# Attention with hash-routed experts: routing computed beside the first batch, row tables three pairs behind their one-hots

## The chip, the cores and the metric

The kernel runs on one core of one Trainium2 chip. The metric is the device time of one launch in microseconds, the median over several runs. A core has TensorE (PE: matmuls and transposes), VectorE (DVE), ScalarE (ACT), GpSimd (POOL) and SyncE (SP); each works through its own list of instructions in the order in which they were written down, and waits where an input or a buffer isn't ready. Loads and stores are started by SP, ACT or POOL and carried out by 16 DMA engines.

## What is computed

```python
B, H, S, D = 8, 8, 576, 64            # attention, block-causal with blocks of 64
scores = (q @ k^T) / sqrt(D);  mask = (row // 64) >= (col // 64)
x = softmax(masked scores) @ v        # -> x: [4608, 512], a row per token

E, F = 8, 1024                        # experts: 512 -> 1024 -> 512
expert_idx = token_ids * 2654435761 % E
out[rows of e] = relu(x[rows of e] @ w1[e]) @ w2[e]
```

Inputs are 32-bit floats, the token ids 64-bit integers. The multiplier is odd, and the kernel needs only the lowest three bits of each id: as 2654435761 leaves the remainder 1 when divided by 8, the expert is the id modulo 8.

## The kernel before

The kernel has two stages. The attention works on **pairs of heads**: 8 batches of 4 pairs, 32 pairs in all, numbered g = 4b + pr. The experts follow, once x has been written to device memory.

For one pair, the chain is as follows. Q and K are loaded as 32-bit values, cast to bf16 (`cast_qk`: rows 0 to 511 on VectorE, the "rest" rows 512 to 575 on GpSimd), transposed on TensorE (`T_pair`, L231; the rest rows of a whole batch by `T_rest`, L206) and copied from PSUM into `qkT` by VectorE (L236, L212). `S_chunk` (L243 to L289) makes the scores of a pair in three chunks, and ScalarE turns each chunk into exponentials `pt` (L289). `S_rest` does the same for the rest rows of a batch. `PV` (L326) multiplies them with V, to which a column of ones is added so that the row sums come with the product, and `norm` (L343, L346) divides by these sums on VectorE. V is cast by GpSimd (`cast_v`, L183 to L188, and `cast_v4`, L194). `write_x` sends a finished batch to `x_dram` from GpSimd's queue.

The order is written out by hand in one loop over g. In step g, the scores of pair g are interleaved with PV of pair g-2; then come the transposes of pair g+2, V casts of pair g+3, one routing step, and the casts of Q and K of the next batch. PSUM for the output of PV exists once (`psO`, one buffer), so PV of a pair waits for the norm of the one before it. The tiles for transposes, `psT`, rotate through two buffers, and the small routing products use them too. Loads go to SyncE's queue; each of Q, K and V has two 32-bit buffers, so a load for batch b+2 starts when batch b has been cast.

**The routing** (`route`, a generator whose parts are separated by `yield`) finds for every token a slot in a table sorted by expert. Its parts are: the expert of each token (L373 to L386, with a small transposing matmul at L381); the one-hot over experts (L394); a running count and the counts per expert, with two matmuls (L400 to L411); the overflow arithmetic, which moves tokens beyond the 640 slots of an expert into extra tiles (L415 to L436); the split of each slot into a column and a lane, `shi` and `slo` (L440 to L448); and the list of overflow tiles (L452 to L462). `rows` prepares row numbers in two digits, `vhi` and `vlo` (L467 to L481).

**The row table** says which row of x belongs in which slot. For each batch, `place_a` makes one-hots of the lanes and columns on VectorE (L490, L493) and multiplies the latter with the row digits on GpSimd (L496, L499). `place_b` multiplies the two on TensorE (L509) and adds the product to `acc` (L512). `placed` turns the sum into the index table `perm3`, by which the experts' rows are gathered and written. Where the steps stand in the loop is given by the dictionary `steps`: routing parts at the end of g = 2 to 8, `rows` at 7, `place_a` of batch j at 11 + 2j, `place_b` at 12 + 2j, `placed` at 27.

After the loop, the rows of each expert are gathered from `x_dram`, transposed, multiplied with w1 and w2, and written to their places. This part isn't touched by the diff. The functions that are:

Of the kernel before, what the change touches and what calls it, by code (L numbers as in the profile page):

```python
# [7 lines left out]
ALU = mybir.AluOpType  # L8
# [12 lines left out]
B, H, S, D = 8, 8, 576, 64  # L21
E, DM, FF = 8, 512, 1024
N = B * S
NT = 4
NP = H // 2
CAP = 640
# [8 lines left out]
def kernel(  # L35
# [10 lines left out]
    nc = tc.nc  # L46
    P = nc.NUM_PARTITIONS
# [49 lines left out]
    def load_qk(b, h0=0, h1=H, rest=True, main=True, engs=None):  # L97
        if b not in loaded:
            loaded[b] = [ld.tile([P, 36, D], F32, name="qf", tag="qf"),
                         ld.tile([P, 36, D], F32, name="kf", tag="kf"), None]  # L100
        for w, src in ((0, q), (1, k)):
            t = loaded[b][w]
            eng = engs[w] if engs else nc.sync
            if main and w == 0:
                eng.dma_start(
                    t[:, 4 * h0 : 4 * h1, :].rearrange("p (h c) d -> p h (c d)", c=4),
                    src[b, h0:h1, 0:512, :].rearrange("h (p c) d -> p h (c d)", c=4),
                )
            elif main:
                for r in range(2):  # L110
                    eng.dma_start(
                        t[:, 4 * h0 : 4 * h1, :].rearrange(
                            "p (h r c) d -> p h r (c d)", r=2, c=2)[:, :, r],
                        src[b, h0:h1, 256 * r : 256 * r + 256, :].rearrange("h (p c) d -> p h (c d)", c=2),
                    )
            if rest:
                for g in range(2):
                    eng.dma_start(
                        t[64 * g : 64 * g + 64, 32:36, :],
                        src[b, 4 * g : 4 * g + 4, 512:576, :].rearrange("h r d -> r h d"),  # L120
                    )
# [41 lines left out]
    def cast_qk(b, which, r0=0, r1=NP, rest=True):  # L163
        src = loaded[b][which]
        cb = casted.setdefault(b, {})
        if which not in cb:
            cb[which] = att.tile([P, 36, D], BF16, name="qb" if which == 0 else "kb",
                                 tag="qb" if which == 0 else "kb")
        dst = cb[which]
        if r1 > r0:  # L170
            nc.vector.tensor_copy(  # L171
                dst[:, 8 * r0 : 8 * r1, :].rearrange("p (r c m) d -> p r m c d", c=4, m=2),
                src[:, 8 * r0 : 8 * r1, :].rearrange("p (r m c) d -> p r m c d", c=4, m=2),
            )
        if rest:
            nc.gpsimd.tensor_copy(dst[:, 32:36, :], src[:, 32:36, :])
# [13 lines left out]
    def cast_v4(b):  # L190
        vf = loaded[b][2]
        vx, v4 = vexts[b % 2]
        for m in range(2):
            nc.gpsimd.tensor_copy(  # L194
                v4[64 * m : 64 * m + 64, :, m, 0:D], vf[64 * m : 64 * m + 64, 32:36, :])
# [165 lines left out]
    tid = rt.tile([B, S], I64, name="tid")  # L361
# [8 lines left out]
    def route():  # L370
# [8 lines left out]
        for i in range(5):  # L379
# [8 lines left out]
        T = 5 * B  # L388
# [30 lines left out]
        inc = rt.tile([P, E], F32, name="inc")  # L419
        nc.vector.tensor_tensor_scan(inc[:], ovf[:], ovf[:], 0.0, op0=ALU.add, op1=ALU.bypass)  # L420
        e640 = rt.tile([P, E], F32, name="e640")
        nc.vector.tensor_single_scalar(e640[:], iota_e[:], float(CAP), op=ALU.mult)

        off1 = rt.tile([P, E], F32, name="off1")
        nc.vector.tensor_tensor(out=off1[:], in0=base[:, 0, :], in1=offs[:], op=ALU.subtract)
        off2 = rt.tile([P, E], F32, name="off2")
        nc.vector.tensor_tensor(out=off2[:], in0=inc[:], in1=ovf[:], op=ALU.subtract)
        nc.vector.tensor_scalar(off2[:], off2[:], 128.0, float(E * CAP - CAP), op0=ALU.mult, op1=ALU.add)
        nc.vector.tensor_tensor(out=off2[:], in0=off2[:], in1=e640[:], op=ALU.subtract)
        nc.vector.tensor_tensor(out=cum[:], in0=cum[:], in1=off1[:, :, None].to_broadcast([P, E, T]), op=ALU.add)  # L430
        ovm = rt.tile([P, E, T], F32, name="ovm")
        nc.vector.tensor_single_scalar(ovm[:], cum[:], float(CAP) + 0.5, op=ALU.is_gt)
        nc.vector.tensor_tensor(out=ovm[:], in0=ovm[:], in1=off2[:, :, None].to_broadcast([P, E, T]), op=ALU.mult)
        nc.vector.tensor_tensor(out=cum[:], in0=cum[:], in1=ovm[:], op=ALU.add)
        nc.vector.tensor_tensor(out=cum[:], in0=cum[:], in1=e640[:, :, None].to_broadcast([P, E, T]), op=ALU.add)
        nc.vector.scalar_tensor_tensor(out=cum[:], in0=cum[:], scalar=-1.0, in1=oh[:],  # L436
                                       op0=ALU.add, op1=ALU.mult)
        yield
        slf = rt.tile([P, T], F32, name="slf")
        nc.vector.tensor_reduce(slf[:], cum[:].rearrange("p e t -> p t e"), axis=AX.X, op=ALU.add)  # L440
# [45 lines left out]
    def place_a(b):  # L486
        ohp = rt.tile([P, 5, P], BF16, name="ohp", tag="ohp", bufs=2)
        ohs = rt.tile([P, 5, NG], BF16, name="ohs", tag="ohs", bufs=2)
        ohg = rt.tile([P, 5, 2, NG], BF16, name="ohg", tag="ohg", bufs=2)
        nc.vector.tensor_tensor(  # L490
            out=ohp[:], in0=iota_p[:, None, :].to_broadcast([P, 5, P]),
            in1=slo[:, b, :, None].to_broadcast([P, 5, P]), op=ALU.is_equal)
        nc.vector.tensor_tensor(  # L493
            out=ohs[:], in0=iota_p[:, None, 0:NG].to_broadcast([P, 5, NG]),
            in1=shi[:, b, :, None].to_broadcast([P, 5, NG]), op=ALU.is_equal)
        nc.gpsimd.tensor_tensor(  # L496
            out=ohg[:, :, 0, :], in0=ohs[:],
            in1=vhi[:, b, :, None].to_broadcast([P, 5, NG]), op=ALU.mult)
        nc.gpsimd.tensor_tensor(  # L499
            out=ohg[:, :, 1, :], in0=ohs[:],  # L500
            in1=vlo[:, :, None].to_broadcast([P, 5, NG]), op=ALU.mult)
        places[b] = (ohp, ohg)

    def place_b(b):
        ohp, ohg = places.pop(b)
        pq = psT.tile([P, 512], F32, name="pq", tag="tp")
        for i in range(5):
            n = P if i < NT else 64
            nc.tensor.matmul(pq[:, 0 : 2 * NG], lhsT=ohp[0:n, i, :],  # L509
                             rhs=ohg[0:n, i, :, :].rearrange("p w g -> p (w g)"),  # L510
                             start=(i == 0), stop=(i == 4))
        nc.vector.tensor_tensor(out=acc[:].rearrange("p w g -> p (w g)"),  # L512
                                in0=acc[:].rearrange("p w g -> p (w g)"), in1=pq[:, 0 : 2 * NG], op=ALU.add)
# [26 lines left out]
    NPAIRS = B * NP  # L540
    both = (nc.sync, nc.scalar)
    load_qk(0, 0, 2, rest=False, engs=both)
    load_qk(0, main=False, engs=both)
    load_qk(0, 2, 8, rest=False, engs=both)
    load_v(0)
    nc.sync.dma_start(tid[:], moe_token_ids.rearrange("(b s) -> b s", b=B))
    load_qk(1)
    load_v(1)
    rgen = route()
# [3 lines left out]
    for w in range(2):  # L553
        cast_qk(0, w, 0, 0)
    T_rest(0)
    for w in range(2):
        cast_qk(0, w, 1, 2, rest=False)

    steps = {g: (lambda: next(rgen, None)) for g in range(2, 9)}
    steps[7] = rows  # L560
    for j in range(B):
        steps[11 + 2 * j] = lambda j=j: place_a(j)
        steps[12 + 2 * j] = lambda j=j: place_b(j)
    steps[27] = placed
    for g in range(NPAIRS + 2):
        b, pr = divmod(g, NP)
        live = g < NPAIRS
        nxt = live and b + 1 < B
        if live:
            S_chunk(g, 0)  # L570
        if g >= 2:
            PV(g - 2, 0)
        if live:
            S_chunk(g, 1)
        if g >= 2:
            PV(g - 2, 1)
            norm(g - 2)
        if live:
            S_chunk(g, 2)
            if pr == 0:  # L580
                S_rest(b)
        if g == 0:
            T_pair(1)
        if g < 2:
            for w in range(2):
                cast_qk(0, w, g + 2, g + 3, rest=False)
        if g + 2 < NPAIRS:
            T_pair(g + 2)
        for gv in range(NP) if g == 0 else (g + 3,):
            bv, pv = divmod(gv, NP)  # L590
            if bv < B:
                cast_v(bv, pv)
                if pv == 0:
                    cast_v4(bv)
        if g in steps:
            steps[g]()
        if nxt:
            if pr == 0:
                cast_qk(b + 1, 0, 0, 2)
            elif pr == 1:  # L600
                cast_qk(b + 1, 1, 0, 2)
            elif pr == 2:
                T_rest(b + 1)
                cast_qk(b + 1, 0, 2, 4, rest=False)
            else:
                cast_qk(b + 1, 1, 2, 4, rest=False)
        if pr == 1 and b >= 1:
            write_x(b - 1)
        if pr == (1 if b == 0 else 0) and b + 2 < B:
            load_qk(b + 2)  # L610
            load_v(b + 2)
        if 6 <= g < 6 + 2 * G:
            nc.gpsimd.memset(xgs[g - 6][:], 0.0)
        if pr == 0 and b == 6:
            load_w1(0)
        if pr == 0 and b == 7:
            load_w2(0)
# [161 lines left out]
```

The softmax here doesn't subtract the row's maximum and nothing guards it: scores larger than these inputs give would overflow.

## Time and profile before

| what | value |
|---|---|
| median of 3 runs | 345.86 us (343.06 to 347.33) |
| profiled span | 343.6 us |
| first exponential of the attention | 9.96 us |
| last exponential starts its run of five at | 152.66 us |
| first gather of expert rows | 171.27 us |
| busy: PE, DVE, ACT, POOL | 81%, 46%, 42%, 58% |

The page divides the span into 40 slices. Below, each digit is the busy share of a slice in tenths, and PEclk is the clock that was granted to TensorE, in tenths of the full one:

```profile
PE   1574784998878888895039989999999999999991
DVE  4345769888868788863020224040413324040330
ACT  1342762887657577783004440604133140604100
POOL 3065378388988789960374647274664737232352
PEclk9997886999989899997558999999999999999998
DMA  7999997899898984672226987796969697825432
```

The attention fills the first 18 slices and a part of the next. In the first six of these, none of TensorE, VectorE, ScalarE and GpSimd is full. From the twenty-second slice on, TensorE is full with the experts' matmuls. In a list in order of time, each row has the start in us, the time in us, the engine, the line, the operation, what it writes and reads, and in brackets how long the engine sat idle before it and what released it. In a table of windows, each row has the window, its length, the busy time of each engine with the number of instructions, the mean granted clock, the share of the DMA engines and the rate.

### The profile page before, as it was taken

Reading aid. Unit: us, or ns where it says so; the run is one execution under the profiler, and the core shown is the slowest. Engines: PE = TensorE matmul, PEld = TensorE weight load, DVE = VectorE, ACT = ScalarE, POOL = GpSimd, SP = SyncE. Lnnn points to the kernel's source line nnn. Section 1 sums busy time; section 2 is a strip of 40 time slices with the busy share of each in tenths; the row PEclk is TensorE's granted clock in tenths of the full one; section 3 lists DMA queues with packets and bytes.
Section 4 is the critical chain, followed back from the end, with each engine's and each line's share of the span. In section 5 each row is a group of like instructions: output and inputs, shape, how many; then the busy total and the mean of one; then the engine's idle time right before and its main releaser. Section 6 shows DMA issues by size and latency. Waiting matters only on the chain. (4 is left out here: it accounts for less than half of the span.)

```text
span 343.6 us, 7894 instructions
## 1 busy us (share of the span) xinstructions
PE 277.1 (81%) x3247; PEld 201.2 (59%) x3247; DVE 158.8 (46%) x346; ACT 142.8 (42%) x169; POOL 198.1 (58%) x281
## 2 busy tenths in 40 slices
PE   1574784998878888895039989999999999999991
PEld 1342663776656666664028865949586685949540
DVE  4345769888868788863020224040413324040330
ACT  1342762887657577783004440604133140604100
POOL 3065378388988789960374647274664737232352
PEclk9997886999989899997558999999999999999998
DMA  7999997899898984672226987796969697825432
GB/s 200 284 272 283 246 273 173 216 280 268 211 288 184 285 184 78 138 134 72 69 85 126 215 194 240 167 215 176 200 203 186 231 175 225 194 77 134 129 130 75
DMA packets 67045, 64.58 MB, mean 188 GB/s; under 512 B 19378, under 2 KB 60340, under 8 KB 64960
## 3 DMA queue, kind: packets, MB, share of 16 engines
q0 software_dynamic: 12288, 35.71, 43.5%
q1 hardware_dynamic: 52064, 27.17, 32.4%
q10 hardware_dynamic: 2656, 1.18, 1.3%
q8 instruction: 26, 0.43, 0.5%
q14 instruction: 11, 0.09, 0.1%
HBM read 67.15 MB, written 15.20 MB: 240 GB/s over the span
## 5 line engine op out<-in xcount | busy, mean ns | idle before, releaser
L289 ACT ACTIVATE pt<-ps 128x1024 bf16<-128x1024 f32 x96 | 94.3, 1022 | 54.3 <-PE ps L265 54.0
L662 ACT ACTIVATE hT<-hp 128x640 bf16<-128x640 f32 x64 | 45.0, 703 | 117.1 <-PE hp L657 117.1
L657 PE MATMUL hp<-xT,w1b 128*128 128x320 bf16 x512 | 72.7, 303 | 0.6 <-DVE xT L646 0.6
L657 PEld LDWEIGHTS <-w1b 128*128 128x128 bf16 x512 | 69.9, 144 | 3.2 <-issue 1.1
L672 PE MATMUL yp<-w2b,hT 128*128 128x512 bf16 x320 | 70.2, 379 | 0.0
L679 POOL DMA_INDIRECT out_dram<-ysb,perm x40 | 39.7, 992 | 35.6 <-DVE ysb L677 26.8
L646 DVE COPY xT<-tpx 128x512 bf16<-128x512 bf16 x40 | 15.7, 422 | 79.4 <-PE tpx L645 77.4
L672 PEld LDWEIGHTS <-hT 128*128 128x128 bf16 x320 | 31.0, 98 | 36.2
L677 DVE COPY ysb<-yp 128x512 f32<-128x512 f32 x40 | 27.7, 692 | 51.7 <-PE yp L672 51.7
L633 POOL DMA_INDIRECT xg<-x_dram,perm x40 | 40.6, 1015 | 16.5 <-issue 11.9
L326 PE MATMUL O<-vx,pt 128*128 128x65 bf16 x896 | 43.7, 206 | 2.6 <-DVE xs L346 2.2
L243 PE MATMUL ps<-qkT 64*128 64x64 bf16 (+2 forms) x384 | 37.9, 280 | 2.6 <-ACT pt L289 2.2
L326 PEld LDWEIGHTS <-pt 128*128 128x128 bf16 x896 | 35.8, 105 | 6.4 <-issue 1.8
L183 POOL CAST vx<-vf 128x512 bf16<-128x512 f32 x32 | 21.1, 669 | 20.9 <-DMA vf<-in_v_dram 19.9
L645 PE MATMUL tpx<-identbf,xg 128*128 128x128 bf16 x160 | 15.0, 229 | 19.9 <-DMA xg<-x_dram,perm 16.7
L356 POOL DMA_DIRECT2D x_dram<-xs x32 | 23.3, 734 | 13.1 <-DVE xs L346 12.6
L346 DVE TENSOR_TENSOR xs<-O,rs 128x320 bf16<-128x320 f32 x64 | 28.4, 486 | 1.1
L265 PE MATMUL ps<-maskq,maskk 64*128 64x64 bf16 (+1 forms) x256 | 28.3, 214 | 0.0
L645 PEld LDWEIGHTS <-xg 128*128 128x128 bf16 x160 | 11.0, 101 | 23.7 <-DMA xg<-x_dram,perm 18.0
L236 DVE COPY qkT<-tp 128x1024 bf16<-128x1024 bf16 x32 | 22.0, 688 | 5.0 <-PE tp L231 4.0
L531 POOL DMA_DIRECT2D w1b<-in_moe_w_dram x8 | 4.9, 614 | 30.8 <-PE tpx L645 26.7
L231 PE MATMUL tp<-identbf,qb 128*128 128x128 bf16 x128 | 13.7, 233 | 8.2 <-DVE qb L171 8.0
(112 smaller groups left out, 264.3 us busy)
## 6 DMA issues: line engine op xcount, KB each, us to landing
vf<-in_v_dram SPq DMA_DIRECT2D x16, 512.0 KB, 7.1
w1b<-in_moe_w_dram POOLq DMA_DIRECT2D x8, 1024.0 KB, 8.1
w2b<-in_moe_w_dram POOLq DMA_DIRECT2D x8, 1024.0 KB, 8.6
qf<-in_q_dram SPq DMA_DIRECT2D x7, 1024.0 KB, 7.9
kf<-in_k_dram SPq DMA_DIRECT2D x14, 512.0 KB, 7.1
x_dram<-xs POOLq DMA_DIRECT2D x32, 128.0 KB, 5.8
qf<-in_q_dram SPq DMA_DIRECT2D x16, 64.0 KB, 6.7
vf<-in_v_dram SPq DMA_DIRECT2D x16, 64.0 KB, 5.8
```

What stands on the lines that cost most here:

```text
L243: nc.tensor.matmul(ps[:, m, o0 : o0 + n], lhsT=qk[rows, pr, 1, 128 * kt : 128 * kt + 128], rhs=qk[rows, pr, 0, q0 : q0 + n], start=first, ...
L265: nc.tensor.matmul(ps[:, m, o0 : o0 + 128 * n].rearrange("p (t h j) -> p t h j", h=2, j=16)[:, :, 0, :], lhsT=maskk[rows, c, :], rhs=maskq ...
L289: nc.scalar.activation(ptv[:, :, 512 * ch : 512 * ch + 512], ps[:], ACT.Exp, scale=SCALE)
L326: nc.tensor.matmul(O[:, t, :], lhsT=pt[:, m * PTW + o0 : m * PTW + o0 + 128], rhs=vx[:, h, i, :], start=(n == 0), stop=(n == t),)
L346: nc.vector.tensor_tensor(out=xs[:, :, 0:DM].rearrange("p t (d h k) -> p h t d k", d=4, h=H)[:, h], in0=O[:, m, :, 0:D].rearrange("p t (k ...
L633: nc.gpsimd.indirect_dma_start(out=xgs[g % (2 * G)][:], out_offset=None, in_=x_dram[:, :], in_offset=bass.IndirectOffsetOnAxis(ap=perm3[:, ...
L645: nc.tensor.transpose(out=tp[:, db, :], in_=xg[:, db * P : (db + 1) * P], identity=identbf[:])
L657: nc.tensor.matmul(hp[:, t, 0:HC], lhsT=w1b[:, db, ft::NFT], rhs=xT[:, db, t * HC : (t + 1) * HC], start=(db == 0), stop=(db == NKT - 1),)
L662: nc.scalar.activation(hT[:, ft, :].rearrange("p (t n) -> p t n", t=2), hp[:, :, 0:HC], ACT.Relu)
L672: nc.tensor.matmul(yp[:], lhsT=hT[:, ft, tt * P : (tt + 1) * P], rhs=w2b[:, ft, :], start=(ft == 0), stop=(ft == NFT - 1),)
L677: nc.vector.tensor_copy(ysb[:], yp[:])
L679: ins = nc.gpsimd.indirect_dma_start(out=out[:, :], out_offset=bass.IndirectOffsetOnAxis(ap=perm3[:, gg : gg + 1], axis=0), in_=ysb[:], in ...
```

## The change

Four things are changed. The token ids are loaded on ScalarE's queue right after the first K rows instead of behind V on SyncE's. The routing parts are brought forward: the first three into step 0, the overflow arithmetic to the end of step 1, the split into columns and lanes to step 2, and the overflow list and `rows` to step 3. The purpose is to use the time in which VectorE waits for the first batch's loads. The overflow arithmetic is fused: the constant -1 is folded into two small operations, and the comparison with the capacity and the multiplication become one operation.

The row tables start earlier, `place_a` of batch j at 5 + 2j, and `place_b` follows at 8 + 2j, three pairs later instead of one, so that TensorE doesn't reach the product before its factors are ready. Last, the casts of Q and K for the next batch, with the rest rows on GpSimd, and the routing steps now stand ahead of the V casts in each step of the loop, so that the rest casts don't queue behind V casts that wait for their load. In step 0, `cast_v4` comes after the V casts.

```diff
-        nc.vector.tensor_single_scalar(e640[:], iota_e[:], float(CAP), op=ALU.mult)
+        nc.vector.tensor_scalar(e640[:], iota_e[:], float(CAP), -1.0, op0=ALU.mult, op1=ALU.add)
...
-        nc.vector.tensor_single_scalar(ovm[:], cum[:], float(CAP) + 0.5, op=ALU.is_gt)
-        nc.vector.tensor_tensor(out=ovm[:], in0=ovm[:], in1=off2[:, :, None].to_broadcast([P, E, T]), op=ALU.mult)
+        nc.vector.scalar_tensor_tensor(
+            out=ovm[:], in0=cum[:], scalar=float(CAP) + 0.5,
+            in1=off2[:, :, None].to_broadcast([P, E, T]), op0=ALU.is_gt, op1=ALU.mult)
...
-        nc.vector.scalar_tensor_tensor(out=cum[:], in0=cum[:], scalar=-1.0, in1=oh[:],
-                                       op0=ALU.add, op1=ALU.mult)
+        nc.vector.tensor_tensor(out=cum[:], in0=cum[:], in1=oh[:], op=ALU.mult)
...
     load_qk(0, 0, 2, rest=False, engs=both)
+    nc.scalar.dma_start(tid[:], moe_token_ids.rearrange("(b s) -> b s", b=B))
     load_qk(0, main=False, engs=both)
     load_qk(0, 2, 8, rest=False, engs=both)
     load_v(0)
-    nc.sync.dma_start(tid[:], moe_token_ids.rearrange("(b s) -> b s", b=B))
...
-    steps = {g: (lambda: next(rgen, None)) for g in range(2, 9)}
-    steps[7] = rows
+    steps = {g: [] for g in range(NPAIRS + 2)}
+    steps[1].append(lambda: next(rgen))
+    steps[2].append(lambda: next(rgen))
+    steps[3] += [lambda: next(rgen, None), rows]
     for j in range(B):
-        steps[11 + 2 * j] = lambda j=j: place_a(j)
-        steps[12 + 2 * j] = lambda j=j: place_b(j)
-    steps[27] = placed
+        steps[5 + 2 * j].append(lambda j=j: place_a(j))
+        steps[8 + 2 * j].append(lambda j=j: place_b(j))
+    steps[23].append(placed)
...
         if g == 0:
+            next(rgen)
+            for w in range(2):
+                cast_qk(0, w, 1, 2, rest=False)
             T_pair(1)
+            next(rgen)
...
-        for gv in range(NP) if g == 0 else (g + 3,):
-            bv, pv = divmod(gv, NP)
-            if bv < B:
-                cast_v(bv, pv)
-                if pv == 0:
-                    cast_v4(bv)
-        if g in steps:
-            steps[g]()
+        if g == 0:
+            next(rgen)
+            for pv in range(NP):
+                cast_v(0, pv)
+            cast_v4(0)
...
+        for step in steps[g]:
+            step()
+        bv, pv = divmod(g + 3, NP)
+        if 0 < bv < B:
+            cast_v(bv, pv)
+            if pv == 0:
+                cast_v4(bv)
```

More of the change, by code (lines that the diff above doesn't have):

```diff
@@ L427, in route @@
         nc.vector.tensor_tensor(out=off2[:], in0=inc[:], in1=ovf[:], op=ALU.subtract)
-        nc.vector.tensor_scalar(off2[:], off2[:], 128.0, float(E * CAP - CAP), op0=ALU.mult, op1=ALU.add)
+        nc.vector.tensor_scalar(off2[:], off2[:], 128.0, float(E * CAP - CAP - 1), op0=ALU.mult, op1=ALU.add)
         nc.vector.tensor_tensor(out=off2[:], in0=off2[:], in1=e640[:], op=ALU.subtract)
@@ L555 @@
     T_rest(0)
-    for w in range(2):
-        cast_qk(0, w, 1, 2, rest=False)
-    steps = {g: (lambda: next(rgen, None)) for g in range(2, 9)}
-    steps[7] = rows
+    steps = {g: [] for g in range(NPAIRS + 2)}
+    steps[1].append(lambda: next(rgen))
+    steps[2].append(lambda: next(rgen))
+    steps[3] += [lambda: next(rgen, None), rows]
     for j in range(B):
-        steps[11 + 2 * j] = lambda j=j: place_a(j)
-        steps[12 + 2 * j] = lambda j=j: place_b(j)
-    steps[27] = placed
+        steps[5 + 2 * j].append(lambda j=j: place_a(j))
+        steps[8 + 2 * j].append(lambda j=j: place_b(j))
+    steps[23].append(placed)
     for g in range(NPAIRS + 2):
```

## The prediction

> **What bounds the kernel now.** I read the span stage by stage first (busy time by windows whose borders are the starts of the first exponential of pairs 0, 8, 12 and 28, and the end of pair 31's last), then the list of waits, then the order in time of ScalarE, of TensorE and of GpSimd around the longest waits. The chain of waits holds only the last 1.1 us of the kernel and says nothing of the attention.
>
> ```profile
> core 0: us, PE busy (x) PEld busy (x) DVE busy (x) ACT busy (x) POOL busy (x), PEclk, DMA share, GB/s
> 9.50:62.00 52.50, 34.04 (x513) 23.45 (x509) 33.38 (x77) 24.37 (x27) 29.59 (x56) 0.84 1.04 245
> 62.00:76.00 14.00, 13.11 (x281) 10.09 (x282) 12.13 (x31) 12.13 (x14) 8.32 (x14) 1.00 1.13 279
> 76.00:144.60 68.60, 59.41 (x1150) 43.87 (x1148) 55.03 (x113) 48.03 (x54) 58.97 (x90) 0.95 0.87 207
> 144.60:157.50 12.90, 11.66 (x265) 8.87 (x262) 7.88 (x19) 11.97 (x14) 6.60 (x10) 1.00 0.70 143
> 157.50:343.60 186.10, 156.79 (x1043) 113.61 (x1039) 45.60 (x86) 44.99 (x65) 91.93 (x99) 0.93 0.65 160
> ```
>
> A batch is four pairs. The last batch, with nothing beside it, takes 12.9 us, and ScalarE is busy 93% of it: that is the pace of a clean pair, 3.2 us. Pairs 8 to 11 take 14.0 us with the DMA engines full. Pairs 12 to 27, which carry the row-table one-hots, take 68.6 us, 17.15 a batch, with no engine full. Pairs 0 to 7 take 52 us where eight clean pairs would take 26. So between 9.5 and 144.6 us the bound is waits in the fixed order of each engine, above a DMA floor; the last 186 us (tail, gather and experts) are not touched by the diff.
>
> ```profile
> ACT pt L289 <- PE ps L265: 54.0, 54, 6.3
> POOL vx L183 <- DMA vf<-in_v_dram: 19.9, 3, 8.1
> PEld L509 <- issue: 9.2, 9, 1.8
> PE pq L509 <- POOL ohg L499: 8.0, 8, 1.7
> ```
>
> The exponentials wait 54.0 us for scores. Eight of the waits behind that are TensorE standing at the first row-table matmul (L509) until GpSimd has multiplied the one-hot: 8.0 us, and the next score matmuls are queued behind it. In the order in time the three long ones are:
>
> ```profile
> 34.31 1.02 ACT L289 ACTIVATE pt<-ps 128x1024 bf16<-128x1024 f32 x1 [6.19 <-PE ps L265]
> 44.33 1.02 ACT L289 ACTIVATE pt<-ps 128x1024 bf16<-128x1024 f32 x1 [2.54 <-PE ps L265]
> 57.86 1.02 ACT L289 ACTIVATE pt<-ps 128x1024 bf16<-128x1024 f32 x1 [6.26 <-PE ps L265]
> ...
> 29.58 0.97 POOL L183 CAST vx<-vf 128x512 bf16<-128x512 f32 x1 [6.10 <-DMA vf<-in_v_dram]
> 32.77 0.40 POOL L176 CAST kb<-kf 128x256 bf16<-128x256 f32 x1
> 43.45 0.17 PE L408 MATMUL pb<-cnt,lower 128*128 128x8 bf16 x1 [2.25 <-DVE cnt L406]
> 56.13 0.61 PE L231 MATMUL tp<-identbf,kb 128*128 128x128 bf16 x4 [5.33 <-DVE kb L171]
> ```
>
> Pair 3 (34.31) waits for the transposes of batch 1's rest rows; their K cast is at 32.77 on GpSimd, behind V casts that waited 6.1 us for V. Pair 5 (44.33) waits behind the count matmul. Pair 7 (57.86) waits for a K cast that VectorE reaches only at 55.39, behind the overflow chain of 48.58 to 55.4.
>
> **What the skill says.** "TensorE: Matmul & The Clock Gate", section "HAM oscillation", says that idle gaps above about 3.4 us drop TensorE to half clock; the trace agrees: 0.84 over pairs 0 to 7, where the 6 us gaps are, 1.00 in the last batch. "SBUF — State Buffer", section "SBUF: two separate sides", says that VectorE with two SBUF inputs and GpSimd exclude each other for a whole instruction; the trace agrees: a two-input operation on 320 elements takes 0.49 us while GpSimd only issues transfers (L430) and 0.78 to 1.33 beside its casts (L433 to L436). "DMA: Bandwidth & Descriptors", section "Issuing engines are not separate DMA queues", says that both queues share 16 engines, so the ids on ScalarE's queue only change the order; no run shows that landing yet.
>
> **The change part by part.** *Ids earlier.* 36 KB go ahead of K's rest rows: one issue, 0.55 us in SyncE's row. It may delay K's rows by 0 to 0.5 us; I take 0.3. *First routing step*, ids to expert table: 28.25 to 31.15 before, 2.9 us on VectorE. It moves to 9.4, where VectorE waited 4.05 us for K until 14.21: hidden, if the ids landed by 9.4. If they land as late as 14 the step costs 3. *One-hot and counts*: 0.48 for L394, and 41.84 to 43.85 for scan, counts, matmul and copy, 2.0. They now stand ahead of pair 1's scores on TensorE, so 2.5 us plus the 0.3: pair 1's first exponential goes from 18.09 to 21.1. Two of the three are given back at once: VectorE then waited until 20.47 for batch 1's Q. The next waits are K and Q of pair 3, so pair 2 starts at 25.0 instead of 23.98.
>
> *Overflow chain*: before, nine small operations 1.5 us and six large ones 5.3. One large operation is fused away and another loses nothing but its scalar, so five remain, 0.49 each beside an idle GpSimd, 0.78 beside a busy one: 2.5 to 3.9, in all 4.0 to 5.4. It now runs at 25.7, once K of batch 1 is cast, and GpSimd waits for V until 29.6, so I take 4.3: to 30.0. Behind it stand the norm of pair 0 (to 31.1) and with it pair 1's PV. *Rest casts ahead of V casts*: K's rest rows land about 27.5 (issued by 21.4, 6.0 to land), cast by 28, transposed by 28.9; pair 3's first exponential at 29.7 instead of 34.31. From there VectorE is the chain: norm 0 to 31.1, qkT 4 and rest copies 32.3, Q cast 33.0, row split 2.2 to 35.2, norm 1 to 36.3, qkT 5 and K cast 37.7, overflow list and row values 1.8 to 39.5, norm 2 to 40.6. Scores of pair 5 come behind transposes that need the 37.7 cast and PV 2, which needs norm 1: 40.7 instead of 44.33. Pairs 5, 6 and 7 then cost 3.6 each: norm 1.11, qkT 0.69, cast 0.69 and half of a one-hot step, (0.9 + 0.6 + 0.3)/2 = 0.9, are 3.4 on VectorE. Pair 8 starts at 51.5 instead of 62.0: **10.5 us gained**.
>
> *Row tables three pairs behind.* The 8.0 us at L509 go: the one-hot of step j is asked for at the end of pair 5+2j and used at 8+2j, 10 us later for 3.4 us of work (1.5 VectorE, 1.88 GpSimd). Two buffers suffice, since the third one-hot is written one pair after the first was read. The ScalarE waits at odd pairs 13 to 27 sum to 15.0 us (1.35, 2.00, 2.50, 1.65, 2.26, 1.65, 1.82, 1.72), which is the most this edit can return. But the work stays. Per batch VectorE needs 4 × (1.11 + 0.69 + 0.69) + 0.49 + 2 × 1.8 = 14.0 us; GpSimd was busy 16.45 of 17.3 us in a batch with one-hots and buffer clears, clears being four of 0.53; DMA moves 3.54 MB of loads and 0.59 of x per batch, 15.0 us at the 275 GB/s of the full slices. Loads of batches 2 and 3 ran full before, so they do not come earlier than about 57. I take 15.5 us for pairs 8 to 15 (GpSimd, DMA), 15.0 for 16 to 19, 14.1 for 20 to 23 and 13.7 for 24 to 27, where one-hots are over: 15.5 + 15.5 + 15.0 + 14.1 + 13.7 = 73.8 instead of 14.0 + 68.6 = 82.6: **8.8 us gained**. Pairs 28 to 31, tail and experts are as before.
>
> Sum: 10.5 + 8.8 = 19.3 us, from the median of 345.86: 326.5.
>
> **The rivals.** *Waits vanish fully.* Pairs 8 to 19 at 14.0 a batch and 20 to 27 at 13.0, as in the clean stages: 68 instead of 82.6, gain 14.6, with the start 25 us: 321. For it: neither VectorE nor TensorE is full between 76 and 144.6, and gaps under 3.4 us keep the clock up. Against it: GpSimd at 95% in a batch, and the DMA slices. *Start alone.* The loads or GpSimd are the true pace, the wait at L509 only hid them; pairs 8 to 27 keep 82.6 and the gain is 10.5: 335.4. For it: DMA share 0.99 between 80.3 and 97.6. Against it: 207 GB/s over the whole stage, against 279 in the stage before. *Routing blocks the start.* The ids land late, the overflow chain ahead of norm 0 holds PV and the x writes, and every pair is the 3 us later that pair 1 is, with batches unchanged because later loads follow later casts: 349, slower than before. For it: VectorE is in order and everything that follows needs it. Against it: the longest waits of pairs 3 and 7 have causes that the new order removes.
>
> **How the numbers follow.** Forecast 0.58, waits vanish 0.17, start alone 0.16, routing blocks the start (from no change to 349) 0.09. The range reaches from 318 (below the second by a faster start, two pairs at 3.2 instead of 3.6 and less contention) to 337 (start alone, with the overflow chain at 5.4). 2% lies at 338.9: faster 0.89, within 2% 0.07, slower 0.04.
>
> **What would show it.** The ids' masking on VectorE near 9.5 with no wait before it; the overflow chain at 25 to 31 with large operations near 0.49; pair 3's first exponential near 30, pair 5's near 41, pair 8's near 51; no wait at L509's successor, and its matmuls between others; GpSimd over 90% busy and the DMA share near 1 from pair 8 to 16; last exponential near 138 in place of 157.5. I am wrong if the first VectorE routing step waits for ids, if V casts wait for V in each batch (DMA-paced), or if the odd pairs still show waits of 2 us at scores.

## The result and the profile after

The changed kernel takes 332.88 us (median of 4 runs, 332.41 to 334.23). Beside it, the kernel before took 346.25. The ratio is 0.9638, with a 95% interval of 0.9578 to 0.9698: 3.6% faster. The forecast was 326.5 us, the range 318 to 337.

The experts' stage, from the last exponential to the end, took 186 to 189 us in the runs around this result and in e5 to e8, but 199 to 208 us in e1 to e4 and e9 to e12, where the kernel before took 360.04 and 365.55 us. So each experiment is read by its ratio to the kernel before in the same runs, and by the time at which its last exponential ends. Only e5 to e8 stand beside a run of the changed kernel; the others are set against profiles of other runs. Where the code is the same, these agree: pairs 0 to 7 take 42.6 us in e2 and 42.7 in the changed kernel, 52.6 in e1 and 52.0 in the kernel before. The profile of e12 is of a slow run, so only its first 26 us are read.

The page of the changed kernel, in 40 slices of 8.3 us:

```profile
PE   1438599889898999960298899999999999999990
DVE  4377979979798878540112041332304133230340
POOL 2083708999999999614764374573737547041452
PEclk9999789979799999995579999999999999999997
DMA  6999999999998987652249986879879697726431
```

GpSimd now stands at 9 from the eighth slice to the sixteenth. The DMA engines are full to the twelfth, without the dips that were there before. TensorE's clock still falls in several slices. By stages (the first window starts at 9.5 us; the other borders are the first exponential of pairs 8, 12, 16, 20, 24 and 28, and the end of the last exponential; the DMA share is the packets' time over that of 16 engines, so packets that overlap can bring it above 1):

```profile
9.50:55.20 45.70, 32.02 (x521) 22.33 (x522) 34.92 (x87) 24.43 (x27) 20.67 (x42) 0.93 1.09 265
55.20:72.60 17.40, 15.32 (x291) 11.51 (x288) 14.25 (x29) 12.02 (x14) 17.05 (x27) 0.90 1.06 267
72.60:89.20 16.60, 15.23 (x292) 11.34 (x290) 14.15 (x29) 12.07 (x14) 16.22 (x26) 0.90 0.97 254
89.20:104.45 15.25, 13.91 (x292) 10.49 (x289) 13.52 (x29) 11.96 (x14) 14.87 (x24) 1.00 0.92 247
104.45:118.75 14.30, 13.74 (x292) 10.49 (x289) 12.21 (x27) 11.96 (x14) 13.95 (x22) 1.00 0.97 263
118.75:132.00 13.25, 12.87 (x281) 9.83 (x278) 10.53 (x26) 11.94 (x14) 12.90 (x21) 1.00 0.82 177
132.00:144.94 12.94, 11.66 (x266) 8.90 (x263) 7.16 (x16) 11.96 (x14) 7.49 (x12) 1.00 0.77 165
144.94:331.00 186.06, 156.12 (x1043) 113.08 (x1039) 45.57 (x86) 45.00 (x65) 91.95 (x99) 0.93 0.65 160
```

The last exponential ends at 144.94 instead of 157.50, 12.56 us earlier, and the span is 12.6 us shorter (331.0 for 343.6): the whole gain lies in the attention. 6.8 us of it are there at pair 8 (first exponential at 55.2 for 62.0). The rest comes between pairs 12 and 27: 59.4 us instead of 68.6, less 3.4 us that pairs 8 to 11 lose (17.4 for 14.0).

The waits between 9.5 and 150 us (who waited for whom, total us, times, longest):

```profile
ACT pt L289 <- PE ps L265: 40.4, 51, 8.4
POOL ohg L496 <- DVE ohs L493: 10.7, 1, 10.7
POOL vx L183 <- DMA vf<-in_v_dram: 9.1, 2, 5.9
PE tp L206 <- POOL kb L176: 6.7, 4, 3.6
PE pq L509 <- DVE qkT L236: 1.1, 2, 0.6
```

The wait of the row-table product for GpSimd (8.0 us) is gone from the list. TensorE now waits for the rest casts of K (L206; 3.1 of the 6.7 us fall on pairs 8 to 27), and 1.1 us at L509 for a copy of VectorE, on whose PSUM buffer the product depends. At pair 10 it waits for both rest casts, which stand on GpSimd behind the one-hot products, V casts and a clear:

```profile
65.77 0.28 PE L206 MATMUL tp<-identbf,qb 128*128 128x128 bf16 x2 [0.99 <-POOL qb L176]
67.13 0.28 PE L206 MATMUL tp<-identbf,kb 128*128 128x128 bf16 x2 [1.07 <-POOL kb L176]
```

The start in order of time (start, us, engine, line, and in brackets the idle time before with its cause):

```profile
10.55 0.40 POOL L176 CAST kb<-kf 128x256 bf16<-128x256 f32 x1 [3.56 <-DMA kf<-in_k_dram]
11.44 0.49 DVE L212 COPY qkT<-tp 128x256 bf16<-128x256 bf16 x2 [4.05 <-PE tp L206]
11.85 0.44 DVE L373 TENSOR_SCALAR ei<-tid 8x576 int32<-8x576 int32 x1
18.22 0.85 DVE L394 TENSOR_TENSOR oh<-et,iota_e 128x320 f32<-128x320 f32 x1
21.89 1.19 DVE L400 TENSOR_TENSOR_SCAN cum<-oh 128x320 f32<-128x320 f32 x1
23.55 0.19 PE L408 MATMUL pb<-cnt,lower 128*128 128x8 bf16 x1 [2.31 <-DVE cnt L406]
24.41 1.94 ACT L289 ACTIVATE pt<-ps 128x1024 bf16<-128x1024 f32 x2 [8.42 <-PE ps L265]
```

VectorE did find the ids when it came to them (11.85, no wait). But it came late, because K's rest rows, cast at 8.03 before, are cast at 10.55. Pair 1's first exponential is at 24.41, 6.3 us later than before, and pair 3's at 32.31, 2.0 us earlier. That lead is lost again: pairs 4, 5 and 6 start 0.7, 1.3 and 0.4 us later than before (39.0, 45.7 and 48.8). The 6.8 us at pair 8 come at pair 7 alone, which starts at 52.1 instead of 57.9 and takes 3.1 us instead of 4.1: its K cast no longer stands behind the overflow chain.

### The profile page after: what moved, and what is told of

The parts are those of the page before. It is cut to its first block, busy times and chain, and to the rows that moved or that the text cites. A ratio compares the mean times of both kernels' runs of the same rounds, so it can differ in the third digit from the quotient of the medians.

```text
span 331.0 us, 7905 instructions
## 1 busy us (share of the span) xinstructions
PE 272.5 (82%) x3247; PEld 198.8 (60%) x3247; DVE 156.2 (47%) x345; ACT 142.6 (43%) x169; POOL 197.4 (60%) x281
## 3 DMA queue, kind: packets, MB, share of 16 engines
q10 hardware_dynamic: 2672, 1.22, 1.5%
## 5 line engine op out<-in xcount | busy, mean ns | idle before, releaser
L641 POOL DMA_INDIRECT xg<-x_dram,perm x40 | 40.6, 1015 | 16.6 <-issue 11.9
L326 PE MATMUL O<-vx,pt 128*128 128x65 bf16 x896 | 41.6, 200 | 6.6 <-DVE xs L346 6.6
L326 PEld LDWEIGHTS <-pt 128*128 128x128 bf16 x896 | 33.8, 102 | 10.3 <-DVE xs L346 5.0
L243 PE MATMUL ps<-qkT 64*128 64x64 bf16 (+2 forms) x384 | 37.1, 275 | 2.8 <-ACT pt L289 2.4
L183 POOL CAST vx<-vf 128x512 bf16<-128x512 f32 x32 | 22.7, 715 | 9.6 <-DMA vf<-in_v_dram 9.1
L653 PEld LDWEIGHTS <-xg 128*128 128x128 bf16 x160 | 11.0, 102 | 24.1 <-DMA xg<-x_dram,perm 18.4
L236 DVE COPY qkT<-tp 128x1024 bf16<-128x1024 bf16 x32 | 22.0, 688 | 7.1 <-PE tp L231 6.0
L231 PE MATMUL tp<-identbf,qb 128*128 128x128 bf16 x128 | 13.8, 235 | 8.0 <-DVE qb L171 8.0
```

What stands on the lines that cost most here:

```text
L243: nc.tensor.matmul(ps[:, m, o0 : o0 + n], lhsT=qk[rows, pr, 1, 128 * kt : 128 * kt + 128], rhs=qk[rows, pr, 0, q0 : q0 + n], start=first, ...
L326: nc.tensor.matmul(O[:, t, :], lhsT=pt[:, m * PTW + o0 : m * PTW + o0 + 128], rhs=vx[:, h, i, :], start=(n == 0), stop=(n == t),)
L641: nc.gpsimd.indirect_dma_start(out=xgs[g % (2 * G)][:], out_offset=None, in_=x_dram[:, :], in_offset=bass.IndirectOffsetOnAxis(ap=perm3[:, ...
L653: nc.tensor.transpose(out=tp[:, db, :], in_=xg[:, db * P : (db + 1) * P], identity=identbf[:])
```

## The experiments

### One part of the change at a time (e1, e2, e3)

e1 takes the kernel before and moves the products alone:

```diff
-        steps[12 + 2 * j] = lambda j=j: place_b(j)
+        steps[14 + 2 * j] = lambda j=j: place_b(j)
-    steps[27] = placed
+    steps[29] = placed
```

> The kernel before with only the lag: row-table products three pairs behind their one-hots (one-hots at 11+2j as before, products at 14+2j, table closed at 29). Own theory (the waits at the product vanish, and GpSimd's work of about 16 us a batch with clears and 14 without sets the pace in their place): pairs 12 to 31 take 73 us instead of 81.5, so about 338 us. Rival (the lag is the whole gain of the change): 333. Rival (loads set the pace, the wait only hid them): 344 to 346.

Measured: 352.65 to 358.42 us against 356.42 to 362.32, which the spread of the runs doesn't tell apart; last exponential at 155.00, 2.5 us earlier than in the kernel before. My 8 us were wrong. The rival of loads was nearer in size, but the trace doesn't name loads. The wait at L509 for GpSimd is gone, and the two waits of TensorE below have come or grown (waits of pairs 12 to 27; L206 for VectorE is new, L231 for the K cast had 1.0 us):

```profile
ACT pt L289 <- PE ps L265: 17.3, 27, 3.2
PE tp L206 <- DVE qkT L236: 3.3, 4, 0.8
PE tp L231 <- DVE kb L171: 2.5, 5, 0.6
```

ScalarE's wait fell only from 20.8 to 17.3 us. TensorE, no longer stopped at the product, stops at transposes instead, for VectorE. By itself the lag mostly moves a wait.

e2 takes the changed kernel and puts the row tables back where they were:

```diff
-        steps[5 + 2 * j].append(lambda j=j: place_a(j))
-        steps[8 + 2 * j].append(lambda j=j: place_b(j))
-    steps[23].append(placed)
+        steps[11 + 2 * j].append(lambda j=j: place_a(j))
+        steps[12 + 2 * j].append(lambda j=j: place_b(j))
+    steps[27].append(placed)
```

> The changed kernel with the row tables where they were before (one-hots at 11+2j, products at 12+2j), so early routing and the new order of casts alone. Own theory (the start is worth the 6.8 us by which pair 8 comes earlier in the changed kernel, and the waits at the product come back): 339.5 us, pair 8 near 55, some 2 us waits of ScalarE at odd pairs 13 to 27. Rival (the start only moves the wait to the loads of batches 2 and 3): 343 or more.

Measured: ratio 0.9864 (0.9759 to 0.9968), last exponential at 153.22, 4.3 us earlier than before. Pair 8 starts at 55.0, as in the changed kernel; the product waits 10.8 us for GpSimd again. The start and the new order are worth about 4 us without the lag, of the 7 that pair 8 had.

e3 keeps everything but the place of the V casts:

```diff
+        (V casts of pair g+3 here, ahead of the casts of Q and K)
         if nxt:
...
         for step in steps[g]:
             step()
-        (V casts of pair g+3)
```

> The changed kernel with the V casts put back ahead of the rest casts and the routing steps in each pair after the first. Own theory (TensorE waits at the rest transposes at pairs 2, 6, 10, 14, 18, 22 because GpSimd reaches the K rest cast late; V casts in front make each of these waits 1 to 2 us longer): 337 to 341 us. Rival (GpSimd's throughput sets the pace whatever the order inside a pair): 333 to 335.

Measured: ratio 0.9793 (0.9689 to 0.9898), last exponential at 149.31, 4.4 us later than in the changed kernel. The order of rest and V casts does count, but not at the start: pair 8 starts at 54.9, for 55.2. The loss comes in pairs 8 to 27, which take 81.5 us instead of 76.8. The waits for the rest cast of K there are only a little longer, 4.4 us for 3.1, so my path explains only a part of it.

By itself the lag gives 2.5 us and start and order together give 4.3; all parts joined give 12.6. Where the other 5.8 us come from isn't shown: the changed kernel also starts its one-hots six pairs earlier, and no run has the early start and the lag with the one-hots at 11 + 2j. That each part takes away a wait behind which another one stands, so that they count only together, is the reading that e1's trace suggests. The earlier routing parts and the fused arithmetic have no run of their own; as e2 and e3 both keep the lead at pair 8, they are its likely source.

### What holds pairs 8 to 19 (e4 to e7, e9 to e11)

The forecast had 15.5 us for each of the first two batches there. They take 17.4 and 16.6, with GpSimd busy 98% and the DMA engines near full. e4 and e6 take work from GpSimd in this stretch, the ten clears:

```diff
-        if 6 <= g < 6 + 2 * G:
-            nc.gpsimd.memset(xgs[g - 6][:], 0.0)
...
+    for xg in xgs:                          # e4: ahead of the loop
+        nc.gpsimd.memset(xg[:], 0.0)
...
+        if 28 <= g < 33:                    # e6: at the end of pairs 28 to 32
+            for z in range(2):
+                nc.gpsimd.memset(xgs[2 * (g - 28) + z][:], 0.0)
```

> The changed kernel with the ten clears of the gather tiles (0.52 us each on GpSimd) moved from the ends of pairs 6 to 15 to the start, where GpSimd waits for V. Own theory (GpSimd, busy 17.05 of 17.4 and 16.22 of 16.6 us, sets the pace of pairs 8 to 15): pairs 8 to 15 take 30.5 us instead of 34.0, about 329.5 us. Rival (the DMA engines, with a share of 1.06 and 0.97 there, set it): 333, no change, and GpSimd waits for V or K instead.

> The changed kernel once more, unaltered, beside the next three, so that they can be compared with it on one chip. Every theory: the last exponential near 145 us, a ratio to the kernel before of 0.955 to 0.97.

> The changed kernel with the ten clears of the gather tiles moved to the ends of pairs 28 to 32, where GpSimd is busy 7.5 of 12.9 us. Own theory (GpSimd is the pace of pairs 8 to 15): 2 to 3 us faster than the changed kernel beside it, pairs 8 to 15 in 31.5 us instead of 34.0. Rival (loads are the pace, since the rate there is 254 to 267 GB/s at a share near 1): less than 1 us faster, GpSimd waits for V or K.

Measured: e4 has the ratio 0.956 (0.947 to 0.9651) and its last exponential at 143.23; e5, the changed kernel again, 0.9621 (0.955 to 0.9692) and 145.13; e6 0.9608 (0.9537 to 0.968) and 144.26. In e4 pairs 8 to 15 take 32.6 us, in e6 32.0, against 34.0 in e5. So the clears are worth 1.4 to 2.1 us in the stage where they stood, less than I had put down. The end moves by 1 to 2 us and the time not measurably: GpSimd is one limit there, and not the only one.

e7 takes the V loads of batches 2 to 7 away:

```diff
             load_qk(b + 2)
-            load_v(b + 2)
+            loaded[b + 2][2] = loaded[b][2]
```

> The changed kernel without the V loads of batches 2 to 7: these batches use the V of batch 0 or 1, so that a quarter of all loaded bytes is gone and nothing else (6 of 24 MB-sized loads). The output differs from the reference's. Own theory (GpSimd and VectorE are the pace of pairs 8 to 15, loads only from pair 16 on if at all): pairs 8 to 15 as in the changed kernel within 1 us, last exponential at most 2 us earlier. Rival (loads are the pace from pair 8 to 27): pairs 8 to 27 in 66 to 68 us instead of 76.8, 9 us faster.

Measured: ratio 0.9641 (0.9546 to 0.9736), last exponential at 143.57. Pairs 8 to 15 take 33.2 us, at a DMA share of 0.60 to 0.74, and pairs 8 to 27 take 77.2, not 66 to 68. The rival that loads set the pace of this stretch is refuted.

e9 moves the V casts between rest casts and routing steps, since the wait of 10.7 us at L496 had V casts and x writes queued behind it on GpSimd:

```diff
-        for step in steps[g]:
-            step()
         (V casts of pair g+3)
+        for step in steps[g]:
+            step()
```

> The changed kernel with the V casts of each pair moved between the rest casts and the routing steps, so that GpSimd's first one-hot product at pair 5, for which it waits 10.7 us idle, no longer stands ahead of the V casts of batch 2. Own theory (GpSimd loses this wait and then runs 17 of 17.4 us behind it, which shows as the wait of 3.1 us at the rest transposes of pair 10): that wait under 1.5 us, pairs 8 to 11 in 15.5 to 16.5 us instead of 17.4, 1 to 2 us faster than the changed kernel (332.7). Rival (loads are the pace there): no change, GpSimd waits for V instead.

Measured: ratio 0.9587 (0.9522 to 0.9651), last exponential at 146.10. The wait at the rest transposes of pair 10 is gone, as I had said. But the row-table product now waits 1.8 us there for the copy of VectorE (L236), and pairs 8 to 11 take 17.8 us, not 15.5 to 16.5. e10 joins this edit, e6 and e8 (below); e11 also leaves the V loads out:

> Three edits on the changed kernel together: count matmul behind the scores of pair 1, clears at pairs 28 to 32, V casts between rest casts and routing steps. Each alone left or should leave the total within 2 us. Own theory (GpSimd and the loads are two floors close together, each hides the other): pair 8 near 51, GpSimd waiting for K and V by pair 16, 329 to 331 us. Rival (the loads alone are the floor from pair 16 on): 333, with all of the lead of pair 8 gone by pair 24.

> The same three edits, and the V loads of batches 2 to 7 left out (these batches use the V of batch 0 or 1, so the output differs). Own theory (taking both floors away at once shows what neither edit alone showed): pairs 8 to 19 at 14.1 us a batch on VectorE, last exponential at 133 to 136, 321 to 324 us. Rival (something else, such as VectorE or the rest transposes, holds the pairs): last exponential at 141 or later, 329 or more.

Measured: e10 0.9638 (0.9585 to 0.9692), last exponential at 145.24; e11 0.9575 (0.9524 to 0.9625), at 144.36. This fells my theory of two floors. With clears, V loads and the order of casts all out of the way, pairs 8 to 11 still take 18.4 us (52.2 to 70.6).

The run e2 bears on this stretch as well. In e2, too, the routing is early and the casts have their new order, but the one-hots begin only at pair 11. It has the clears and all loads, and pairs 8 to 11 take 14.4 us, from 55.0 to 69.4:

```profile
55.00:69.40 14.40, 13.13 (x282) 9.97 (x278) 10.41 (x23) 12.02 (x14) 11.38 (x19) 1.00 0.98 249
```

So what makes these pairs long in the changed kernel is the row-table work that now lies in them, 3 us of it, with loads at the same share. That work takes time on VectorE and GpSimd and needs a `psT` buffer. One way in which it holds up the pairs is seen in the trace of e11, in order of time around pair 10:

```profile
60.31 1.22 DVE L491 TENSOR_TENSOR ohp<-iota_p,slo 128x640 bf16<-128x640 bf16 x1
61.46 0.93 DVE L494 TENSOR_TENSOR ohs<-iota_p,shi 128x360 bf16<-128x360 bf16 x1
62.32 0.21 DVE L343 RECIPROCAL rs<-O 128x10 f32<-128x10 f32 x1
62.56 0.89 DVE L346 TENSOR_TENSOR xs<-O,rs 128x320 bf16<-128x320 f32 x2
63.36 0.68 DVE L236 COPY qkT<-tp 128x1024 bf16<-128x1024 bf16 x1
64.09 0.87 PE L510 MATMUL pq<-ohg,ohp 128*128 128x144 bf16 x5 [1.85 <-DVE qkT L236]
65.55 1.02 ACT L289 ACTIVATE pt<-ps 128x1024 bf16<-128x1024 f32 x1 [2.96 <-PE ps L265]
```

In the third pair of a batch, three tiles pass through the two buffers of `psT`: the pair's transposes, the rest transposes, and the row-table product. The product needs the buffer of the first, and its copy (L236) stands on VectorE behind the one-hots of the step before and a norm. The one-hots take 1.22 and 0.93 us here, beside GpSimd's casts, for 0.80 and 0.52 where GpSimd doesn't cast. So the product waits 1.85 us, and the scores behind it wait too; e9 and e10 have the same wait, of 1.8 and 1.9 us. A slower clock follows (windows of 1 us in e11; busy PE, PEld, DVE, ACT, POOL, then TensorE's clock, DMA share, rate):

```profile
63.00:64.00 1.00, 0.00 (x0) 0.00 (x0) 1.00 (x4) 0.00 (x0) 0.86 (x3) 0.88 0.17 35
65.00:66.00 1.00, 1.00 (x18) 0.89 (x15) 0.42 (x2) 0.45 (x1) 1.00 (x2) 0.50 0.11 26
71.00:72.00 1.00, 1.00 (x27) 0.76 (x25) 1.00 (x2) 1.00 (x2) 0.91 (x1) 1.00 1.11 344
```

The clock is at a half from 63.8 to 70.6 us. TensorE is full from 64.1 on; a group of four score matmuls takes 0.61 us, for 0.39 at full clock, and pair 11 takes 5.0 us. Pairs 10 and 11 together take 10.95 us, pairs 8 and 9 take 7.4, so that 3.5 us go with a wait of 1.85. In the changed kernel the clock is at a half from 67.6 to 71.0 and from 84.6 to 88.1 us, after the waits at pairs 10 and 14.

The length of one gap doesn't decide it, though. At pair 14 e11 has a gap of 1.70 us, and the clock stays up (a row of the list in time, then windows of 3.41 us; the first ends where the clock falls):

```profile
82.07 0.58 PE L510 MATMUL pq<-ohg,ohp 128*128 128x144 bf16 x5 [1.70 <-DVE qkT L236]
60.35:63.76 3.41, 1.89 (x42) 1.45 (x40) 3.38 (x7) 2.24 (x3) 3.23 (x5) 1.00 0.80 190
77.41:80.82 3.41, 2.96 (x66) 2.33 (x65) 3.38 (x6) 3.09 (x4) 2.70 (x5) 1.00 0.08 17
80.82:84.23 3.41, 2.16 (x47) 1.75 (x46) 2.63 (x7) 1.23 (x2) 3.41 (x6) 1.00 0.09 15
```

In the 3.41 us before the fall TensorE was busy for 1.89 us; at pair 14 the gap is spread over two stretches of that length, with 2.96 and 2.16 us. That the busy time of a stretch decides, and not the single gap, is only suggested by this.

That it is this copy that bounds once the other two are relieved, is read from the trace; no run gave `psT` a third buffer or moved the one-hots behind the copy, so it isn't shown by an experiment.

### The start (e8, e12)

e8 puts the count matmul behind the scores and transposes of pair 1:

```diff
+        yield
         pb = psT.tile([P, 5, 65], F32, name="pb", tag="tp")
...
-        if g == 0:
+        if g < 2:
             next(rgen)
+        if g == 0:
```

> The changed kernel with the count matmul and its copy put behind the scores and transposes of pair 1 instead of ahead of them; the scan and counts on VectorE stay. Own theory (TensorE's wait of 2.31 us before the count matmul delays pair 1, but the list of VectorE from 28 to 44 us sets pair 5): pair 1 near 22 instead of 24.4, pair 5 within 0.7 us of 45.7, total within 1 us of the changed kernel. Rival (the delay of pair 1 is carried to the end): 2.3 us faster than the changed kernel beside it.

Measured: ratio 0.9641 (0.9556 to 0.9726), last exponential at 144.98. Pair 1 starts at 22.5. Pair 5 starts at 41.1, not within 0.7 us of 45.7: my reason was wrong, the wait at pair 1 is carried on, and doubles. Yet the total doesn't move. The lead of 4.6 us at pair 8 (50.8 for 55.4 in e5) is still 4.5 at pair 20, 1.3 at pair 24 and 0.2 at pair 28. In between GpSimd waits for loads, at a DMA share of 0.98 in pairs 20 to 23 and 1.08 in 24 to 27:

```profile
111.68 0.40 POOL L176 CAST kb<-kf 128x256 bf16<-128x256 f32 x1 [2.10 <-DMA kf<-in_k_dram]
115.09 0.62 POOL L183 CAST vx<-vf 128x512 bf16<-128x512 f32 x1 [3.01 <-DMA vf<-in_v_dram]
127.78 0.40 POOL L176 CAST kb<-kf 128x256 bf16<-128x256 f32 x1 [1.98 <-DMA kf<-in_k_dram]
```

By this trace loads are a floor after all, but later than the rival put it: for pairs 20 to 27, and for a kernel that gets there 4.5 us earlier. No run with e8's edit takes only loads away.

e12 loads the ids last on ScalarE's queue:

```diff
     load_qk(0, 0, 2, rest=False, engs=both)
-    nc.scalar.dma_start(tid[:], ...)
     load_qk(0, main=False, engs=both)
     load_qk(0, 2, 8, rest=False, engs=both)
+    nc.scalar.dma_start(tid[:], ...)
```

> The changed kernel with the load of the token ids behind all K loads of batch 0 on ScalarE's queue instead of ahead of K's rest rows. Own theory (the ids ahead cost the first exponential 2 us through K's rest rows, but the list of VectorE up to 45 us sets pair 5): first exponential near 10.3 instead of 12.4, pair 5 within 0.7 us of 45.7, total within 1 us. Rival (the start's delay is carried through): 2 us faster than the changed kernel.

Measured: ratio 0.9628 (0.9556 to 0.9699), no different from e5. K's rest rows are cast at 8.12 and the first exponential is at 10.1: the 2.4 us at the start were the ids' doing. But then VectorE waits for the ids:

```profile
9.01 0.49 DVE L212 COPY qkT<-tp 128x256 bf16<-128x256 bf16 x2 [2.13 <-PE tp L206]
14.49 0.45 DVE L373 TENSOR_SCALAR ei<-tid 8x576 int32<-8x576 int32 x1 [4.99 <-DMA tid<-in_moe_token_ids_dram]
```

The delay is only exchanged for another, and pair 1 starts at 25.2, no earlier than in the changed kernel.

## Why the prediction was right, and where it was off

The direction and the range were right. The size was not: 19.3 us were forecast, and the spans differ by 12.6. Both parts of the sum gave about two thirds of what was put down, 6.8 us of 10.5 up to pair 8 and 5.8 of 8.8 in pairs 8 to 27. The two waits that the prediction wanted to remove did go, the product's at L509 and pair 7's for its K cast behind the overflow chain. Beyond the size of each part, adding them up failed, as e8 shows: there the start comes out as forecast (pair 5 at 41.1 for 40.7, pair 8 at 50.8 for 51.5), and the last exponential stays where it was. That the time still lies in the range is owed to its width, which had to hold one of the parts alone. Point by point:

- *Ids earlier, 0.3 us.* Mis-sized: K's rest rows came 2.5 us later. The ids themselves were in time.
- *First routing step hidden.* Right: it is on VectorE from 11.85 to 15.6, with a wait of 1.7 us for its transposing matmul, while K of pair 1 was awaited until 16.48.
- *One-hot and counts.* Pair 1 was put at 21.1 and is at 24.4. 2.2 us of the miss are the rest rows. The durations were taken from a time when GpSimd didn't cast: L394 took 0.85 for 0.48, the scan 1.19 for 0.81, the casts of pair 2 0.83 for 0.42. Pair 2, put at 25.0, starts at 28.2: "Two of the three are given back at once" failed. Pair 5, put at 40.7, starts at 45.7; with the count matmul out of pair 1's way (e8) it is at 41.1.
- *Overflow chain, 4.3 us.* 5.1 (28.77 to 33.85), inside 4.0 to 5.4, for 6.9 before. It came 3 us later than put down, beside V casts, and its large operations took 0.57 to 0.92. In e8 it runs at 27.4, four of the five beside an idle GpSimd at 0.49, and takes 4.2.
- *Rest casts ahead of V casts.* Pair 3 starts at 32.3 for 29.7, about as late as pair 2. The order is worth 4.4 us at the end (e3), but not at the start, where the prediction counted it.
- *Pair 8 at 51.5, 10.5 us gained.* 55.2, 6.8 us gained, and by another path: the forecast had pairs 3 and 5 start 4.6 and 3.6 us earlier, but what pair 3 won was lost again by pair 4, and pair 7 brought all of it. Pairs 5 to 7 cost 3.2 us each, less than the 3.6 put down.
- *The wait at L509 goes.* Right: 8.0 us to none for GpSimd. The lag alone returned 2.5 us of them (e1).
- *15.5, 15.5, 15.0, 14.1, 13.7 us a batch.* Measured: 17.4, 16.6, 15.25, 14.3, 13.25. The first two are 3.0 us short together; the last three fit. "GpSimd, DMA" as the cause was too simple: e6 and e7 each removed some of one, e11 of both, and pairs 8 to 11 stayed at 16.9 to 18.4 us. The row-table work in these pairs costs 3 us more than without it (e2). What the sum lacked, by e11's trace, is the order inside the third pair of a batch, with three tiles for two buffers behind VectorE, and the half clock after such waits.
- *Gaps and the clock.* I had put down that gaps under 3.4 us leave the clock up, as the Trainium skill's "TensorE: Matmul & The Clock Gate", section "HAM oscillation", has it. Here the page and the traces differ: in e11 the clock fell around a gap of 1.85 us and stayed at a half for 6.8 us, and the trace decides. The profile of before had shown it already. No gap of TensorE in pairs 12 to 27 was longer than 1.7 us, and the mean clock there was 0.95: it was at a half from 97.9 to 101.3 us, after a gap of 1.68, and from 115.0 to 118.4, after one of 0.98.
- *The signs of being wrong.* One of the three came in part. ScalarE still waits for scores at pairs 11, 15, 19 and 23, for 3.1, 2.1, 2.1 and 1.1 us: one odd pair in two, in place of every odd pair.

Of the rivals, *waits vanish fully* fell with pairs 8 to 19. *Start alone* fell, since pairs 8 to 27 take 76.8 us and not 82.6, and since e2 lacks the lag and has its last exponential 8.3 us later than the changed kernel. *Routing blocks the start* was true of pairs 1 and 2, 6.3 and 4.2 us late, and in a small way of pairs 4 to 6; pair 7 made it good.

## What to carry to other kernels

When a wait in a fixed order is removed, list what stands next in line: here the rest casts on GpSimd, the copy that frees a PSUM buffer, and the loads came one after the other, and no edit that relieved some of them brought a measurable gain in time. Take the durations for moved work from a stretch in which the neighbours will be as busy as in the new place; some operations of VectorE took twice as long beside GpSimd's casts (0.83 us for 0.42). Gains of two stages can't be added without asking whether the second stage keeps the lead of the first: 4.6 us at pair 8 were nothing at pair 28.

## What the runs showed of the hardware

- In e4, ten clears on GpSimd, which read nothing, took 4.73 us back to back, and a VectorE operation that takes 0.44 us elsewhere took 4.08 beside them; it ended 0.3 us after the last clear. No other run shows it:

```profile
10.49 4.73 POOL L557 MEMSET xg<- 128x512 bf16 x10
11.45 4.08 DVE L373 TENSOR_SCALAR ei<-tid 8x576 int32<-8x576 int32 x1
```

- 36 KB of ids ahead on ScalarE's queue delayed the next small loads there by 2.4 us (cast of K's rest rows at 10.55 with the ids ahead, 8.12 with them behind).
- TensorE's clock fell to a half around idle gaps of 1.85 us in e11 and of 0.98 us in the kernel before, while a gap of 1.70 us in e11 left it up: the length of one gap doesn't decide. It was back after 3.4 us in the changed kernel (at pairs 11 and 15) and after 6.8 us in e11 (at pair 11).
